# A fused attention and two-layer kernel: the hops of each weight rounding set a point apart, and six w_k blocks moved into the mixing phase

## The chip, the cores and the metric

The kernel runs on one core of a Trainium2 chip. The metric is the device time of one execution in microseconds (us), the median of several runs. The engines are TensorE (PE, matrix products), VectorE (DVE), ScalarE (ACT), GpSimd (POOL) and SyncE (SP, which here only issues DMAs). Each works through its own instructions in program order; semaphores hold one until what it needs from the others is there.

## The reference

The inputs pass through three stages. All matrix products are in fp32 to a tight tolerance.

```python
for t in range(S):                               # delta-rule attention, B=4, H=8, S=768, D=48
    y[:, :, t] = einsum('bhd,bhde->bhe', q[:, :, t], state)
    v_old = einsum('bhde,bhd->bhe', state, kt)
    state = state + bt[:, :, :, None] * einsum('bhd,bhe->bhde', kt, vt - v_old)
h = gelu(x @ w_in); u, v = split(h)              # gated mixing over the sequence
v_n = (v - mean) / sqrt(var + 1e-6) * g_ln
x = x + (u * (einsum('ts,bsd->btd', w_sg, v_n) + b_sg)) @ w_out
k = relu(xk @ w_k); v = k * k @ w_v              # xk, xr: x mixed with x one token earlier
out = sigmoid(xr @ w_r) * v
```

## The kernel before, in words

PE multiplies fp32 numbers as pairs of rounded halves (hi and lo, three products each). The weights arrive as 64-bit floats, so each must first be **rounded**, block by block (128 rows by 192, 256 or 384 columns), by the generator `narrow`: a load of the raw bits (L161, on SP), a cast of the low words (ACT, L165), four DVE operations on the tile `na` (L170, L172, L174, L176), an integer add on POOL (L178), then hi on ACT (L121, in `split`) and lo on POOL (L124). `resident` blocks (12 of w_in) stay in on-chip memory; `scratch` blocks (8 of w_out, 12 of w_k, 3 of w_r, 8 of w_v) are put to DRAM (L203) and loaded again later.

The program has four stages. **Early** (to about 42 us): a triangular solver for the first chunk pair (`solver(0)`, nearly all on DVE) runs, with the first w_in roundings beside it; PE waits for it. **Attention** (to about 345 us): the order on every engine is written out by a planner in Python, one `tick` after the other. A tick's `background` hands DVE time in turn to layer-norm steps, steps of the next solver, and rounding steps of the jobs in `running`; `after(n, f)` puts an instruction n points (ticks) later. Five more solvers run here. Each ends in a transpose (L456) into a tile that the program calls DT, or sw0l where it shares memory, and PE's `couple` (L472) needs it at a set place. **Mixing** (to about 494 us): 32 turns of `mix`, whose product PE makes; DVE scales it (L1072), multiplies it by u (L1074), ACT rounds it (gh, L1075), DVE takes the rest (gl, L1078); `project` multiplies the result by w_out. Some turns also bring in a batch's next v tiles (`to_ring`): ACT rounds one into g (L121), DVE or POOL takes the rest (L124). Between, the function `side` gives two DVE steps a turn to the rounding of w_r and w_v, in up to three blocks at a time, one for each raw buffer of the pool `st`. What is left after the last turn is run off in a loop (`while k == 7 ...`) before the next stage. **Last phase**: `shift` makes the token mix xm (L1165, L1166, L121, L124), and PE computes the third stage chunk by chunk. The tiles of `shift` lie in the memory of that pool, so the first xm_hi waits until the last puts from there have landed.

PE's own instructions stand in the same order in both kernels, so only how long it waits, and its clock, can differ.

## Time and profile before

| what | value |
|---|---|
| runs | 741.00, 735.49, 739.16 us; median 739.16 |
| profiled execution | 737.01 us, of which the span that the trace covers is 735.2 us |
| mean granted PE clock | 0.972 of full speed |
| busy | PE 682.0 us (93%), DVE 502.0 (68%), ACT 364.3 (50%), POOL 202.6 (28%) |
| chain that ended last | PE 78%, DVE 10%, "issue" 4%, ACT 4%, DMA 2% |

The span is what the profiler saw between the first and the last instruction; the 1.8 us around it belong to the execution. A busy share is an average over the whole span. Each engine's instructions are listed with their start, their duration and, in brackets, how long the engine had been idle before and what ended that idle time.

### The profile page before, as it was taken

To read this page: it belongs to the slowest core of one execution; us is meant where nothing else is said; L and a number is where in the kernel's file an instruction comes from. 1 tells how busy PE (TensorE), PEld (TensorE's weight loads), DVE (VectorE), ACT (ScalarE), POOL (GpSimd) and SP (SyncE) were. 2 spreads that over 40 slices of the span, in tenths; PEclk is the share of its full clock that TensorE was granted. 3 is DMA by queue.
4 is the path that set the end of the run, shared out by engine and by line. 5 is a ranking of instruction groups with operands and counts; after the bars stand their busy time and mean duration, and the time that the engine had idled before them with its cause. 6 is when DMAs were issued, how large, how long until landed. Compare 5 with 4: busy or idle time off the path is not lost.

```text
span 735.2 us, 24465 instructions
## 1 busy us (share of the span) xinstructions
PE 682.0 (93%) x10669; PEld 618.3 (84%) x10669; DVE 502.0 (68%) x992; ACT 364.3 (50%) x696; POOL 202.6 (28%) x257
## 2 busy tenths in 40 slices
PE   2568889999997998899999999999999999999998
PEld 2436668878886897789999999998989898999997
DVE  5999989978979695723558676798655564736251
ACT  2235676777765766864322323156444453525140
POOL 4033543454444555643041615330000000000000
PEclk8678999999998999999999999999999999999999
DMA  8402654665665458548853444367000000000000
GB/s 246 108 30 72 158 141 121 177 177 178 155 200 179 126 178 219 186 132 232 284 185 132 153 148 150 109 200 186 33 12 23 22 21 22 18 27 11 33 12 32
DMA packets 80938, 88.71 MB, mean 121 GB/s; under 512 B 24704, under 2 KB 63616, under 8 KB 80832
## 3 DMA queue, kind: packets, MB, share of 16 engines
q1 hardware_dynamic: 75520, 77.33, 35.6%
q0 software_dynamic: 5312, 9.83, 5.0%
q8 instruction: 83, 1.36, 0.8%
q14 instruction: 23, 0.19, 0.1%
HBM read 56.60 MB, written 25.82 MB: 112 GB/s over the span
## 4 chain that ended last, share of the span: by engine, by line
PE 78%; DVE 10%; issue 4%; ACT 4%; DMA 2%; POOL 1%; SPq 1%; ACTq 0%; POOLq 0%; DVEq 0%
PE ms L152 34%; PE ms L976 12%; PE ms L703 7%; PE ms L651 6%; PE ms L579 3%; PE rk L537 2%; PE rk L550 2%; PE rk L514 2%; PE sps L565 2%; PE ms L742 2%; PE ms L334 2%; DVE sg L356 2%; PE ms L472 2%; PE qk L517 1%; DVE sg L396 1%
## 5 line engine op out<-in xcount | busy, mean ns | idle before, releaser
L152 PE MATMUL ms<-wvh,sl 128*128 128x384 f32 x192 | 64.7, 337 | 0.5 <-DVE sl L124 0.5
L152 PE MATMUL ms<-wvh,sh 128*128 128x384 f32 x192 | 64.6, 337 | 0.1
L152 PE MATMUL ms<-wvl,sh 128*128 128x384 f32 x192 | 64.5, 336 | 0.0
L178 POOL TENSOR_TENSOR na<-na,raw 128x256 int32<-128x256 int32 (+2 forms) x43 | 38.7, 899 | 93.3 <-ACT gh L1075 40.7
L1075 ACT ACTIVATE gh<-w 128x384 fp32r<-128x384 f32 x32 | 16.8, 526 | 93.7 <-DVE w L1074 93.7
L152 PE MATMUL ms<-xm_hi,sw0h 128*128 128x512 f32 x144 | 56.1, 390 | 0.0
L152 PE MATMUL ms<-xm_hi,sw0l 128*128 128x512 f32 x144 | 56.1, 389 | 0.0
L152 PE MATMUL ms<-xm_lo,sw0h 128*128 128x512 f32 x144 | 56.0, 389 | 0.0
L124 DVE TENSOR_TENSOR sl<-sg,sh 128x512 fp32r<-128x512 f32 x48 | 33.2, 691 | 28.8 <-ACT sh L121 28.6
L976 PE MATMUL ms<-sw0h,g 128*128 128x384 f32 x192 | 50.2, 335 | 0.0
L976 PE MATMUL ms<-ws1h,g 128*128 128x384 f32 x192 | 49.9, 334 | 0.0
L121 ACT ACTIVATE sh<-sg 128x512 fp32r<-128x512 f32 x48 | 30.3, 631 | 33.9 <-DVE sg L1188 33.9
L1205 DVE TENSOR_TENSOR sg<-sg,ms 128x384 f32<-128x384 f32 x24 | 13.3, 552 | 49.4 <-PE ms L152 49.4
L356 DVE TENSOR_TENSOR sg<-sg,Yt 128x512 f32<-128x512 f32 (+4 forms) x72 | 43.3, 611 | 1.3
L530 POOL TENSOR_SCALAR_AFFINE_SELECT SQ<-SQ 64x512 f32<-64x512 f32 x36 | 28.2, 783 | 48.6 <-ACT SQ L529 47.5
L1187 ACT ACTIVATE sg<-ms 128x512 f32<-128x512 f32 x48 | 28.6, 596 | 26.1 <-PE ms L152 24.1
L1188 DVE TENSOR_TENSOR sg<-sg 128x512 f32<-128x512 f32 x48 | 33.2, 691 | 10.9 <-ACT sg L1187 10.8
L334 PEld LDWEIGHTS ms<-kT 64*32 64x32 f32 x640 | 18.5, 124 | 22.4 <-issue 14.5
L703 PE MATMUL ms<-xl,wiu_hi 128*128 128x256 f32 x144 | 37.0, 296 | 0.0
L152 PEld LDWEIGHTS ms<-wvh,sl 128*128 128x128 f32 x192 | 36.1, 188 | 0.8 <-DVE sl L124 0.8
L703 PE MATMUL ms<-xh,wiu_lo 128*128 128x256 f32 x144 | 36.4, 291 | 0.0
L152 PEld LDWEIGHTS ms<-wvh,sh 128*128 128x128 f32 x192 | 36.1, 188 | 0.4 <-ACT sh L121 0.4
(244 smaller groups left out, 2151.0 us busy)
## 6 DMA issues: line engine op xcount, KB each, us to landing
u_d<-ug SPq DMA_DIRECT2D x24, 256.0 KB, 4.0
u<-u_d SPq DMA_DIRECT2D x16, 384.0 KB, 4.1
vn_d<-v SPq DMA_DIRECT2D x22, 256.0 KB, 3.5
vk<-in_vk_dram SPq DMA_DIRECT2D x24, 192.0 KB, 4.0
vk<-in_vk_dram SPq DMA_DIRECT2D x12, 384.0 KB, 3.7
st<-vn_d SPq DMA_DIRECT2D x18, 256.0 KB, 3.1
out_dram<-sg SPq DMA_DIRECT2D x24, 192.0 KB, 1.9
kT<-in_kt_d_dram SPq DMA_DIRECT2D x8, 512.0 KB, 5.3
```

The lines of the kernel that those rows point to most:

```text
L121: A.activation(hi, src, AF.Copy)
L124: eng_lo.tensor_tensor(lo, src, hi.bitcast(F32), op=ALU.subtract)
L152: T.matmul(pt, lhsT=a, rhs=b, start=(i == 0), stop=(i == n - 1))
L178: G.tensor_tensor(a.bitcast(I32), a.bitcast(I32), w_lo.bitcast(I32), op=ALU.add)
L334: T.matmul(gps[r:r + 32, p, c0:c1], lhsT=t[r:r + 64, u, 0:32], rhs=t[r:r + 64, u, c0:c1], start=True, stop=True)
L356: V.tensor_tensor(tv, vw(a_t, a_off, a_dims), vw(b_t, b_off, b_dims), op=ALU.mult)
L530: G.affine_select(out=pt, in_=pt, pattern=[[0, 8], [1, C]], compare_op=ALU.is_gt, fill=0.0, base=0, channel_multiplier=-1)
L651: T.matmul(vstat[g, b], lhsT=a[:, c], rhs=w[:, c], start=first, stop=last)
L703: T.matmul(vstat["u"][:, 2 * P * d:2 * P * d + 2 * P], lhsT=w[:, c, ds_], rhs=a[:, c].rearrange("p b t -> p (b t)"), start=first, stop=last)
L976: T.matmul(pt[:, :DM], lhsT=v[:, ds_], rhs=w, start=(c == 0 and i == 0), stop=(c == 5 and i == 2))
L1187: A.activation(r, pt, AF.Relu)
L1188: V.tensor_tensor(r, r, r, op=ALU.mult)
```

## The change

It has four parts. First, the hops of a rounding: the POOL add, hi and lo each come one point after the one before, in the early stage and in attention (`hops[0]` is 1), where the add came at once and hi and lo together; in mixing `hops[0]` is 0, so add and lo come without such a pause. Second, rounding jobs get DVE time in the order in which they were begun, all of them and not the first two in turn; up to three run in the early stage (there were two), three in attention (two), and a new one begins every eighth point (sixth). Third, the last six w_k blocks are taken out of the attention stage and rounded in mixing, in a lane of their own that goes ahead of the lane of w_r and w_v. Fourth, the scaling of the second value tile (`scale_v(1)`) has a place at the end of the list of pending work, and pending streams keep their due time when points are counted anew.

```diff
-RUN = (3, 2, 3)
+RUN = (3, 3, 3)
-EVERY = 6
+EVERY = 8
+NMIX = 6
...
-        G.tensor_tensor(a.bitcast(I32), a.bitcast(I32), w_lo.bitcast(I32), op=ALU.add)
+        yield hops[0], lambda: G.tensor_tensor(a.bitcast(I32), a.bitcast(I32), w_lo.bitcast(I32), op=ALU.add)
...
-        yield lag, lambda: split(A, G, af, hi, lo)
+        yield 1, lambda: A.activation(hi, af, AF.Copy)
+        yield hops[0], lambda: G.tensor_tensor(lo, af, hi.bitcast(F32), op=ALU.subtract)
...
-    jobs += j1
+    jobs += j1[:-NMIX]
+    wk_jobs = j1[-NMIX:]
...
-                kinds.append([e for e in ready if any(e[1] is j for _, j in running[:2])])
+                kinds.append([e for _, j in running for e in ready if e[1] is j])
...
-                while len(running) < 2 and len(jobs) > n_rest:
-                    start_job(LJ0 if point[0] else LJ)
+                while len(running) < 3 and len(jobs) > n_rest:
+                    start_job(LJ0 if point[0] else (LJ, LJ, 2 * LJ0)[len(running)])
...
-                after(SV, lambda: scale_v(1))
+                last.append(lambda: scale_v(1))
...
+        for e in streams:
+            e[0] = len(later) if e[0] > point[0] else 0
         point[0] = 0
-        for e in streams:
-            e[0] = 0
+        later += [(len(later) + 1, last[0])]
...
-    jobs += j2 + j3
-    live, turns, starts, owing = [], [0], [4 + 2 * i for i in range(NRAW)], []
+    hops[0] = 0
+    live, turns, owing = [], [0], []
+    lanes = [(jobs + wk_jobs, [0] * NRAW), (j2 + j3, [4 + 2 * i for i in range(NRAW)])]
...
-            while jobs and any(x <= turns[0] for x in starts):
-                starts.remove(next(x for x in starts if x <= turns[0]))
-                j = jobs.pop(0)()
-                next(j)
-                live.append([turns[0] + 2, j, None])
-            e = next((e for e in live if e[0] <= turns[0]), None)
+            for q, starts in lanes:
+                while q and any(x <= turns[0] for x in starts):
+                    starts.remove(next(x for x in starts if x <= turns[0]))
+                    j = q.pop(0)()
+                    next(j)
+                    live.append([turns[0] + 2, j, None, starts])
+            e = next((e for _, x in lanes for e in live if e[0] <= turns[0] and e[3] is x), None)
...
-        while k == 7 and (live or jobs):
+        while k == 7 and (live or lanes[1][0]):
```

**ACT in the early stage.** L343 (L345 after) are the four copies of the first Gram product out of PSUM into sg1, which solver 0's first transpose on DVE needs whole; L165 (L164) is the cast of a raw block, L121 (L181) its hi. Before:

```order
L165 ACTIVATE raw_145<-raw_145 128x256
L165 ACTIVATE raw_147<-raw_147 128x256
L343 ACTIVATE sg1_109<-ms_234 128x8x32
L121 ACTIVATE wiv_hi_91<-na_227 128x256
L121 ACTIVATE wiv_hi_91<-na_229 128x256
L343 ACTIVATE sg1_109<-ms_281 128x8x32
```

After:

```order
L164 ACTIVATE raw_145<-raw_145 128x256
L345 ACTIVATE sg1_109<-ms_233 128x8x32
L164 ACTIVATE raw_147<-raw_147 128x256
L345 ACTIVATE sg1_109<-ms_273 128x8x32
L181 ACTIVATE wiv_hi_91<-na_228 128x256
L345 ACTIVATE sg4_112<-ms_315 128x256
```

The fourth copy into sg1 stood behind two hi's, which wait for POOL's adds; now it stands ahead of both.

**DVE at the end of solver 4** (the one whose result TensorE waits for longest). L491 (L493) adds up a chunk's residual r32 and waits for PE; L356 and L396 (L358, L398) are products and sums of the solver; L170 to L176 (L169 to L175) belong to a rounding. Before:

```order
L491 TENSOR_TENSOR r32_4582<-vk_3871,rk_4546 128x384
L356 TENSOR_TENSOR sg3_111<-sg2_110,Yt_144 128x512
L356 TENSOR_TENSOR sg3_111<-sg2_110,Yt_144 128x256
L396 TENSOR_REDUCE sg2_110<-sg3_111 128x4x16
L670 BN_STATS st6_4606<-v_4593 128x6
L356 TENSOR_TENSOR sg3_111<-sg2_110,Yt_144 128x768
L170 TENSOR_SCALAR na_4613<-raw_4597 128x256
L396 TENSOR_REDUCE sg2_110<-sg3_111 128x4x16
L172 TENSOR_SCALAR na_4613<-na_4613 128x256
```

After:

```order
L358 TENSOR_TENSOR sg3_111<-sg2_110,Yt_144 128x512
L358 TENSOR_TENSOR sg3_111<-sg2_110,Yt_144 128x256
L398 TENSOR_REDUCE sg2_110<-sg3_111 128x4x16
L493 TENSOR_TENSOR r32_4542<-vk_3835,rk_4506 128x384
L169 TENSOR_SCALAR na_4558<-raw_4431 128x192
L358 TENSOR_TENSOR sg3_111<-sg2_110,Yt_144 128x768
L171 TENSOR_SCALAR na_4558<-na_4558 128x192
L672 BN_STATS st6_4566<-v_4553 128x6
L398 TENSOR_REDUCE sg2_110<-sg3_111 128x4x16
```

Two products and a sum of the solver that came behind the residual (L356 with 512 and 256 columns and the first L396) come ahead of it; a block of 192 columns stands where one of 256 stood.

**ACT at the end of mixing.** L1075 (L1080) is the last turn's gh, L121 (L181) a block's hi, L165 (L164) a cast, xm_hi the first instruction of the last phase that waits for the blocks' puts. Before:

```order
L1075 ACTIVATE gh_8024<-w_8083 128x384
L1165 ACTIVATE sg1_8167<-xT_63,m1_sb_66 128x512
L1165 ACTIVATE sg2_8168<-xT_63,m1_sb_66 128x512 x2
L1075 ACTIVATE gh_8024<-w_8109 128x384
L121 ACTIVATE raw_7973<-na_8033 128x384
L121 ACTIVATE xm_hi0_8220<-sg1_8167 128x512 x2
```

After:

```order
L1080 ACTIVATE gh_7990<-w_8079 128x384
L181 ACTIVATE raw_7938<-na_7999 128x384
L181 ACTIVATE raw_7940<-na_8057 128x384
L164 ACTIVATE raw_8084<-raw_8084 128x384
L181 ACTIVATE raw_8084<-na_8141 128x384
L164 ACTIVATE raw_8137<-raw_8137 128x384
L181 ACTIVATE raw_8137<-na_8151 128x384
L120 ACTIVATE xm_hi0_8220<-sg1_8167 128x512 x2
```

One block was open behind the last gh; now four are, of which two are not yet cast.

**SP at the end of mixing.** L161 (L160) loads a raw block of w_v, L203 puts a rounded one to DRAM. Before:

```order
L203 DMA wv_d_6887<-raw_7619 128x768
L161 DMA raw_7973<-in_w_v_dram 128x768
L203 DMA wv_d_6887<-raw_7747 128x768
L203 DMA wv_d_6887<-raw_7897 128x768
L203 DMA wv_d_6887<-raw_7973 128x768
```

After:

```order
L160 DMA raw_8084<-in_w_v_dram 128x768
L203 DMA wv_d_6815<-raw_7938 128x768
L160 DMA raw_8137<-in_w_v_dram 128x768
L203 DMA wv_d_6815<-raw_7940 128x768
L203 DMA wv_d_6815<-raw_8084 128x768
L203 DMA wv_d_6815<-raw_8137 128x768
```

The last load stood ahead of the last three puts and had its buffer early. Now the load of raw_8137 stands behind the put of raw_7938, whose buffer it takes over, and waits until that put has landed.

## Rows read from the trace of the kernel before

**Rows 1.** Windows: bounds, length, busy PE, PEld, DVE, ACT, POOL (instructions), PE clock, DMA, GB/s

```profile
80.00:340.00 260.00, 242.97 (x6747) 209.59 (x6739) 199.50 (x427) 177.63 (x347) 126.25 (x166) 0.98 0.60 167
232.80:238.00 5.20, 5.16 (x77) 4.91 (x78) 4.83 (x22) 2.35 (x5) 0.89 (x2) 0.50 0.57 180
340.00:490.00 150.00, 150.00 (x868) 149.27 (x867) 102.36 (x181) 46.78 (x91) 48.54 (x50) 1.00 0.55 177
```

**Rows 2.** Timeline of ACT and DVE, 10 to 16 us: start, duration, instruction, [idle before <- releaser]

```profile
13.82 0.42 ACT L121 ACTIVATE wiv_hi<-na 128x256 fp32r<-128x256 f32 x1 [1.53 <-POOL na L178]
14.14 0.80 ACT L343 ACTIVATE sg<-ms 128x256 f32<-128x256 f32 x2
...
10.50 0.75 DVE L176 SCALAR_TENSOR_TENSOR na<-raw,na 128x256 uint32<-128x256 uint32 x2
14.76 1.25 DVE L361 STREAM_TRANSPOSE sg<-sg 128x1024 f32<-128x1024 f32 x1 [3.51 <-ACT sg L343]
```

**Rows 3.** Timeline of TensorE, 36 to 49 us

```profile
41.97 6.50 PE L742 MATMUL ms<-warm 128*128 128x512 bf16 x18 [5.55 <-DVE warm L452]
```

**Rows 4.** Waits of TensorE, 80 to 345 us: total us, times, longest

```profile
PE ms L472 <- DVE sw0l L456: 3.4, 2, 3.1
PE ms L472 <- DVE DT L456: 1.9, 1, 1.9
...
PE ms L651 <- ACT ug L707: 1.4, 1, 1.4
PE ms L579 <- ACT SQ L556: 1.3, 2, 1.1
```

**Rows 5.** Timeline of DVE, then TensorE, 220 to 235 us

```profile
220.56 0.55 DVE L491 TENSOR_TENSOR r<-vk,rk 128x384 f32<-128x384 f32 x1 [2.70 <-PE qk L517]
221.03 1.48 DVE L356 TENSOR_TENSOR sg<-sg,Yt 128x512 f32<-128x512 f32 x2
222.43 0.67 DVE L396 TENSOR_REDUCE sg<-sg 128x64 f32<-128x512 f32 x1
...
230.85 1.93 DVE L456 STREAM_TRANSPOSE sw0l<-sg 128x1024 f32<-128x1024 f32 x1
...
232.84 1.92 PE L472 MATMUL ms<-sw0l,sw0h 32*32 32x32 f32 x64 [3.08 <-DVE sw0l L456]
```

**Rows 6.** Timeline of ACT, POOL and TensorE, 486 to 495 us

```profile
486.53 0.51 ACT L121 ACTIVATE raw<-na 128x384 fp32r<-128x384 f32 x1
490.96 2.19 ACT L121 ACTIVATE xm_hi<-sg 128x512 fp32r<-128x512 f32 x4 [3.93 <-DMA wv_d<-raw]
...
487.11 1.42 POOL L124 TENSOR_TENSOR raw<-na,raw 128x384 fp32r<-128x384 f32 x1 [3.79 <-ACT raw L121]
...
494.32 0.39 PE L152 MATMUL ms<-xm_hi,sw0h 128*128 128x512 f32 x1
```

**Rows 7.** Chain of waits, 478 to 500 us: start, duration, what

```profile
488.56 2.30 DMA wv_d<-raw
```

**Rows 8.** DMA issues of the span: count, size, median us to landing

```profile
raw<-in_w_v_dram SPq DMA_DIRECT2D x8, 384.0 KB, 3.2
```

**Rows 9.** Windows of the tile na alone: busy us of DVE, ACT, POOL (instructions)

```profile
80.00:340.00 260.00, 40.32 (x92) 9.47 (x24) 37.67 (x48) 0.98 0.60 167
340.00:495.00 155.00, 19.93 (x44) 5.63 (x11) 24.27 (x22) 1.00 0.55 175
```

**Rows 10.** Timeline of DVE, POOL and TensorE, 368 to 382 us

```profile
369.94 1.64 DVE L1078 TENSOR_TENSOR gl<-w,gh 128x384 fp32r<-128x384 f32 x1
...
374.99 0.62 DVE L1072 SCALAR_TENSOR_TENSOR w<-ms,g_sb,b_sb 128x384 f32<-128x384 f32 x1 [0.60 <-PE ms L976]
...
377.31 0.69 DVE L124 TENSOR_TENSOR g<-st,g 128x512 fp32r<-128x512 f32 x1
...
368.31 2.86 POOL L124 TENSOR_TENSOR g<-st,g 128x512 fp32r<-128x512 f32 x2 [18.79 <-ACT g L121]
...
380.86 0.51 PE L976 MATMUL ms<-sw0h,g 128*128 128x384 f32 x2
```

More of the change, by code (lines that the diff above doesn't have):

```diff
@@ L34 @@
 WARM = 4
-SV = 60
 B0 = 1.0
@@ L39 @@
 SOLVE0 = 1
-RUN = (3, 2, 3)
+RUN = (3, 3, 3)
 SUMS = (0,)
-EVERY = 6
+EVERY = 8
+NMIX = 6
 LATE = 100
 PUT = 2
-JLAG = 2
 BUDGET = 1.62
@@ L153, in mm3, with narrow @@
                 i += 1
-    def narrow(dram, i, j, hi, lo, cw=CW, pool=stg, lag=JLAG, parts=None):
+    def narrow(dram, i, j, hi, lo, cw=CW, pool=stg, parts=None):
         w = CW if pool is stg else cw
@@ L190, in resident @@
         return hi, lo, [lambda i=i, j=j: narrow(dram, i, j, hi[:, i, j - j0:j - j0 + CW],
-                                                lo[:, i, j - j0:j - j0 + CW], lag=0)
+                                                lo[:, i, j - j0:j - j0 + CW])
                         for i in range(nblk) for j in range(j0, j1, CW)]
@@ L221, in fused_kernel @@
     wk_dh, wk_dl, j1 = scratch(w_k, "wk", 3, FF)
-    jobs += j1
+    jobs += j1[:-NMIX]
+    wk_jobs = j1[-NMIX:]
     n_rest = len(jobs)
+    hops = [1]
     fp = tc.tile_pool(name="fp", bufs=2)
@@ L819, in fused_kernel @@
                  ((st_n, 0, 0), (st_rq, 1, 0)), ((st_d, 1, 0), (st_s, 0, 0), (st_y, 0, 0))]
-        rest = [lambda j=j: whole(j) for j in diag[4:]]
+        last, rest = [], [lambda j=j: whole(j) for j in diag[4:]]
         k = 0
@@ L1044, in side @@
                 live.remove(e)
-                starts.append(turns[0] + 1)
+                e[3].append(turns[0] + 1)
             elif isinstance(c, tuple) and c[0]:
@@ L1126, in fused_kernel @@
         if k == 6:
+            assert not lanes[0][0] and all(e[3] is not lanes[0][1] for e in live)
             wk = [[None] * 3 for _ in range(2)]
```

## The prediction

> **What bounds the kernel now.** I read the windows first, since the busy shares of the whole span mix stages with different limits. In mixing PE is busy all of the time, 150.00 of 150 us, with DVE at 102.36 [rows 1]: nothing that the other engines gain there shortens anything, and they have to take on a good deal before it costs. From 80 to 340 us PE is busy 242.97 of 260 us, so some 17 us are idle and can be won at most, besides what the clock loses. Before about 42 us PE waits for solver 0 on DVE; the last wait of that stage is 5.55 us, for a DVE instruction inside the solver [rows 3]. So the question of this change is which waits before 340 us it shortens, and what six more blocks do to a mixing stage that had no wait, and to the handover behind it.
>
> The waits from 80 to 345 us name few places [rows 4]: the solver's last transpose (3.4 us in two waits, and 1.9 in one more) and ACT evictions behind others (1.4 and 1.3). The longest, 3.08 us, ends at 232.84 [rows 5]. In the 5.2 us after it PE runs at a granted clock of 0.50, its lower level of 1.2 GHz, and is busy 5.16 of them [rows 1]; at 2.4 GHz that work is 2.6 us. The wait and what the clock did after it cost 3.1 + 2.6 = 5.7 us.
>
> **Early stage.** The solver's first transpose starts at 14.76, when the two last copies into sg have come out of ACT. They stand behind a hi that waited 1.53 us for POOL's add [rows 2]. With the new order the last of them that the transpose needs stands ahead of both hi's. DVE has nothing else then but the rounding that ends at 10.50 + 0.75 = 11.25; the transpose follows a part of it, so I let it begin at 10.6 instead of 14.76, 4.1 us earlier (11.25 would make it 3.5). Against it, the add and lo of the blocks now run beside the solver, which before had waited for them. I take 1.0 us off, from the row of a DVE instruction that ran beside POOL, 1.64 us [rows 10], against 0.69 for a similar one without [rows 10]: one such meeting. **Gain 3.1 us**, bounds 1.5 (three meetings) and 4.1.
>
> **Six blocks fewer in attention.** A block costs DVE four instructions of 40.32 / 92 = 0.44 us, so six are 10.5 us less in the stage, and about 6 x (2 x 0.78) = 9.4 us less of POOL and 6 x 0.39 = 2.4 of ACT [rows 9]. What of it reaches PE is decided at the places where it waits.
> - Solver 4: the residual waits for PE at 220.56, after 2.70 us of DVE idle time [rows 5]. Two products (1.48) and a sum (0.67) that came behind it now fill part of this idle time: 2.15 us earlier. The rounding between has 192 columns instead of 256, a quarter off 4 x 0.44, which is 0.4. That makes 2.6 of the 3.08 us, and what of the wait stays would then be short enough to leave open whether the clock falls. The full price is 5.7, and if only the 2.6 come off and the clock still falls it is 2.6. I take **5.0**, near the full price, because DVE stands idle there for longer than the moved work takes; bounds 1 and 5.7.
> - The other wait on that tile: 3.4 - 3.08 = **0.3** us [rows 4, 5], bounds 0 and 0.3; with fewer DVE steps ahead of it I let it go.
> - Solver 5: its last stretch holds as many rounding steps as before, so its wait of 1.9 [rows 4] stays: **0**, bounds -1 (the transpose comes later as three blocks run at once) and +1.9.
> - From 283 to 330 us: the ACT waits of 1.4 and 1.3 [rows 4] come while rounding instructions queue on ACT and POOL; two blocks fewer there and hops that wait less on ACT: **2.0**, bounds 0 and 2.7.
>
> Together **10.4 us** (with 3.1 from the early stage), bounds 1.5 and 14.7.
>
> **Mixing.** Lane 0 adds 6 x 4 = 24 DVE instructions of 19.93 / 44 = 0.45 us [rows 9], or 10.9 us, to a DVE with 47.6 us free. But it adds them early: twelve of them now stand ahead of the DVE instruction at 377.31, which makes the lo of a v tile, g, that PE first reads with the second of the two products that start at 380.86, so at about 381.0 [rows 10]. Twelve are 5.4 us; the idle 0.60 at 374.99 absorbs that much. The lo is ready at 377.31 + 0.69 + 5.4 - 0.6 = 382.8, or 1.8 us late. Part of DVE's free time must lie ahead of 374.99 too, so I take **1.0** late; bounds 0 and 8.3 (a rival below).
>
> **The handover.** This is the loss that the order shows and no row of before has. In before one block was open behind the last gh: hi at 486.53, lo at 487.11, its put at 488.56 for 2.30 us, and xm_hi at 490.96 after 3.93 us of waiting [rows 6, 7]. PE noticed nothing, since `project` kept it busy until xm was ready at 494.32 [rows 6]. After the change lane 0 has taken the turns that the last two blocks would have used. Behind the last gh, at the same place on ACT, stands the hi of raw_7938, and the load of raw_8137 needs this buffer. So, one after the other: hi 486.53 + 0.51, lo 1.10, put 2.30, load 3.2 [rows 8], four DVE instructions 1.81, add 1.10, hi 0.51, lo 1.10, put 2.30 [rows 6 to 9]; 1.10 is 24.27 / 22. The sum is 13.9 us, and the eight handovers at 0.03 to 0.10 us each (487.11 - 487.04, 490.96 - 490.86) make 0.6. xm_hi can start at 486.53 + 13.9 + 0.6 = 501.0, its first 0.55 us (2.19 / 4) done at 501.6. PE then waits from 494.32 to 501.6, or 7.3 us. Afterwards the clock: 3.08 us of waiting were followed by 5.2 us at 0.50 [rows 1, 5], and I charge the same 2.6 here. **Loss 9.9 us.** Lower bound 6.5, with POOL at its quick end, no slow put, and a clock that recovers at once; upper bound 13, with lo at 1.42 twice [rows 6], load and put a microsecond longer each, and a second stretch at the lower level. The loads of w_r and w_v that wait for the last put are wanted a whole chunk of products later, and I let them cost nothing; if that cover failed they would cost the 3 us or so by which they are late.
>
> The Trainium skill (DMA: Bandwidth & Descriptors, "Anatomy of one DMA") states a fixed part of about 2.0 us for one DMA and a size part of its bytes over 436,000 a microsecond. By it (an estimate from that page) each 384 KB transfer of the chain is 2.9 us, three of them 8.7 where the rows give 7.8, and the loss would be 10.8; the rows decide here, 2.30 and 3.2.
>
> **Sum.** On the profiled execution 737.01: -10.4 + 1.0 + 9.9 = +0.5, so 737.5. That execution lies 2.15 under the median of the runs; moved over to the median 739.16 it is 739.7, and I give **739.5**.
>
> **Rivals.** *Faster: the handover costs its lower bound and the gains come in full.* 6.5 against gains of some 15: DVE's relief takes the whole 3.08 and the clock stretch, and the 1.9 of solver 5 and its aftermath too. -14.7 + 1.0 + 6.5 = -7.2, or 732. For it: DVE is what most of these waits name [rows 4], and 10.5 us of it go. Against: the last stretch of solver 5 has not changed.
>
> *Slower: DVE and POOL block each other in the first mixing turns.* Five more POOL instructions now run before the g split. At 369.94 a DVE instruction took 1.64 us while POOL ran two splits from 368.31 [rows 10]; the longer one at 377.31 took 0.69, so each meeting may cost 1.0. Five make the g split about 5 us later than at best: PE waits some 5.7 us at 381, and at the price above 2.6 more for the clock, 8.3 in place of 1.0. That gives 739.7 + 7.3 = 747. It decides from the third such meeting on, when the wait passes 3 us; for fewer it is hidden in my bounds. Against it: DVE has idle time on both sides of this stretch [rows 1], and POOL's hops here wait for ACT, which thins them out.
> The Trainium skill (SBUF — State Buffer, "Who interferes with whom") says that a DVE instruction with two SBUF inputs contends with a GpSimd instruction that reads SBUF, and that the loser is blocked for the whole instruction. By that rule this rival is the likelier in mixing; the trace agrees at 369.94 only, as far as it shows.
>
> *The change does less than it says:* the waits at solvers 4 and 5 stay, since the transpose waits for something else, and gains are 4; then -4 + 1.0 + 9.9 = +6.9, or 746. I count it with the slower side.
>
> **How the numbers follow.** A measurement of this kernel can tell about 1%, or 7.4 us, from no change. The forecast, gains and losses that nearly cancel: 0.53. The faster rival and what lies beyond it: 0.26. The two slower ones: 0.21, of which a good half passes 1%, but so do combinations of the upper bound of the handover with middling gains. The range of 730 to 747 reaches to both rivals' own times and leaves a tenth out on either side.
>
> **What would show it.** In the profile after: a wait of some 7 us of PE on xm_hi near 500 us (shifted earlier by the gains), with a chain of put, load, DVE, POOL, put before it, and a granted clock of 0.5 behind it; the transpose of solver 0 some 4 us earlier; no wait, or a short one, on the solver 4 transpose and no stretch at 0.50 there; a short wait on DVE's lo of g at the first batch change in mixing. The prediction is wrong if the wait for xm_hi is under 4 us, if the early stage gains nothing, or if PE waits in mixing by more than 3 us.

## The result and the profile after

The changed kernel takes 745.15 us in the median (741.84 to 748.53, nine runs) against 739.16 for the kernel before in the same measurement. The ratio is 1.0076, with a 95% interval of 1.0049 to 1.0103: slower by a little under 1%. The forecast was 739.5, the range 730 to 747. The profiled execution after took 745.61 us, with a span of 743.8 at a mean granted clock of 0.970.

PE's matmuls stand in the same order in both kernels, and either trace holds 10,669 of them. So the two traces can be laid side by side: the start of a matmul after, minus the start of the same matmul before, says how much has been lost or won up to that place. This **shift** is +0.9 us when solver 0's wait ends (42 us), -4.2 at 92, -1.4 at 128, -2.4 at 225, -4.0 at 345, -0.4 from 382 to 494, +9.7 at 498 and +8.6 from 520 to the end. So in these two executions 4.0 us are won before mixing, 3.7 of them are given back in mixing, and 9.0 are lost at the handover. The sum of +8.6 is between two single executions; that of before, 737.01 us, was a quick one, and the medians differ by 6.0.

**The handover.** The windows of the kernel after (bounds, length, then busy PE, PEld, DVE, ACT and POOL with instructions, PE clock, DMA, GB/s) show where the loss is; the first answers to the last window of [rows 1].

```profile
340.00:490.00 150.00, 147.09 (x851) 146.06 (x850) 106.83 (x197) 46.76 (x96) 52.67 (x52) 1.00 0.55 181
...
496.00:507.00 11.00, 5.93 (x14) 4.43 (x15) 4.64 (x9) 5.33 (x10) 4.59 (x6) 0.53 0.94 258
```

From 496 to 507 us PE is busy 5.93 of 11 us. The chain of waits of the kernel after (start, duration, what) tells what it waits for, link by link:

```profile
489.25 3.22 DMA raw<-in_w_v_dram
...
492.56 0.37 DVE na L169
...
493.35 0.97 DVE na L173
...
495.27 1.00 POOL na L177
...
496.90 1.00 POOL raw L182
...
497.92 2.36 DMA wv_d<-raw
...
500.38 0.64 ACT xm_hi L120
```

This is the forecast chain: load, DVE, add, lo, put, xm_hi. Its first links stand on SP's timeline, where the put of the buffer is issued at 486.85 and the load that takes this buffer over only at 489.25, when the put has landed. The end of the chain on the timelines of ACT and TensorE (after the duration, in brackets, the idle time before and what ended it) answers to the xm_hi rows of [rows 6]:

```profile
500.38 2.19 ACT L120 ACTIVATE xm_hi<-sg 128x512 fp32r<-128x512 f32 x4 [3.56 <-DMA wv_d<-raw]
...
501.07 0.80 PE L151 MATMUL ms<-xm_hi,sw0h 128*128 128x512 f32 x1 [6.94 <-ACT xm_hi L120]
```

PE waited 6.94 us (forecast: 7.3). From 496 to 507 the mean granted clock is 0.53, and the same xm matmul takes 0.80 us where it took 0.39 [rows 6]. From 495 to 498 the shift grows by 10.1, of which 3.0 is the clock, and 1.1 comes back by 518, where before had small waits of its own: 9.0 in all.

**Mixing.** Two waits are new. The first was in no part of the prediction. DVE, then TensorE:

```profile
360.42 0.30 DVE L169 TENSOR_SCALAR na<-raw 128x256 uint32<-128x256 uint32 x1 [3.61 <-DMA raw<-in_w_k_dram]
...
360.96 0.61 DVE L1077 SCALAR_TENSOR_TENSOR w<-ms,g_sb,b_sb 128x384 f32<-128x384 f32 x1
...
364.50 0.55 DVE L1083 TENSOR_TENSOR gl<-w,gh 128x384 fp32r<-128x384 f32 x1
...
365.10 0.45 PE L151 MATMUL ms<-gl,wo_hi 128*128 128x384 f32 x1 [1.62 <-DVE gl L1083]
```

The first rounding step of lane 0 comes due before its load has landed. DVE works in order, so for 3.61 us it does nothing, and the scaling of the mixing turn (L1077) behind that step stands too; its gl reaches PE 1.62 us late. The second wait is the forecast one, on the lo of g. POOL, DVE, TensorE:

```profile
378.77 3.23 POOL L123 TENSOR_TENSOR g<-st,g 128x512 fp32r<-128x512 f32 x2 [3.02 <-ACT g L120]
...
379.08 1.77 DVE L123 TENSOR_TENSOR g<-st,g 128x512 fp32r<-128x512 f32 x1
...
380.91 0.62 PE L979 MATMUL ms<-sw0h,g 128*128 128x384 f32 x2 [1.24 <-DVE g L123]
```

DVE's lo of g begins 1.8 us later than in [rows 10] and takes 1.77 us beside POOL's two, where it took 0.69.

**Before mixing.** The waits of TensorE from 80 to 340 us (us in all, times, longest), beside [rows 4]:

```profile
PE ms L474 <- DVE DT L458: 3.5, 3, 1.5
PE ms L653 <- ACT ug L709: 3.0, 2, 2.3
PE ms L474 <- DVE sw0l L458: 2.3, 1, 2.3
```

Solver 4's wait (sw0l) is 2.3 where it was 3.1, and a wait on ug that [rows 4] has only at 1.4 now has a 2.3 in it. That one is new, at 251.5 us: POOL, ACT, TensorE.

```profile
247.94 1.48 POOL L483 TENSOR_TENSOR vk<-vk,neT 128x768 f32<-128x768 f32 x1 [3.86 <-DMA vk<-in_vk_dram]
249.37 1.18 POOL L177 TENSOR_TENSOR na<-na,raw 128x256 int32<-128x256 int32 x1
...
250.58 0.42 ACT L181 ACTIVATE raw<-na 128x256 fp32r<-128x256 f32 x1 [5.23 <-POOL na L177]
250.90 0.58 ACT L709 ACTIVATE ug<-ms 128x512 f32<-128x512 f32 x1
...
251.54 0.50 PE L653 MATMUL ms<-wiv_hi,xh 128*128 128x512 f32 x1 [2.26 <-ACT ug L709]
```

Put a point later, the add of a block (L177) now stands on POOL behind the scaling of a value tile (L483), which itself waits 3.86 us for a DMA. The block's hi on ACT waits 5.23 us for the add, and the eviction that PE needs (ug) stands behind the hi.

In the early stage the rows that answer to [rows 2] and [rows 3] are, of TensorE, ACT, DVE and TensorE:

```profile
13.72 0.21 PE L338 MATMUL ms<-kT 64*32 64x32 f32 x1 [4.82 <-issue]
...
14.44 0.63 ACT L345 ACTIVATE sg<-ms 128x256 f32<-128x256 f32 x1 [4.47 <-PE ms L338]
...
15.11 1.25 DVE L363 STREAM_TRANSPOSE sg<-sg 128x1024 f32<-128x1024 f32 x1 [3.19 <-ACT sg L345]
...
42.86 3.43 PE L744 MATMUL ms<-warm 128*128 128x512 bf16 x8 [5.33 <-DVE warm L454]
```

The copy stands ahead of both hi's now, as the order said, but it waits for PE: the last piece of the first Gram product comes at 13.72. The transpose starts at 15.11 (before 14.76), and PE's wait for solver 0 ends at 42.86 (before 41.97).

### The profile page after: what moved, and what is told of

It reads as the page before. It is cut to its first block, busy times and chain, and to the rows that moved or that the text cites. A ratio compares the mean times of both kernels' runs of the same rounds, so it can differ in the third digit from the quotient of the medians.

```text
span 743.8 us, 24469 instructions
## 1 busy us (share of the span) xinstructions
PE 682.0 (92%) x10669; PEld 618.6 (83%) x10669; DVE 508.0 (68%) x992; ACT 363.9 (49%) x696; POOL 205.2 (28%) x257
## 4 chain that ended last, share of the span: by engine, by line
PE 67%; DVE 20%; DMA 5%; issue 4%; ACT 2%; SPq 1%; POOL 1%; ACTq 0%; DVEq 0%; POOLq 0%
PE ms L151 36%; PE ms L979 8%; PE ms L705 6%; PE ms L653 5%; DVE sg L358 4%; DVE sg L398 2%; PE ms L581 2%; PE rk L539 2%; PE sps L567 2%; PE rk L552 1%; PE rk L516 1%; DMA vk<-in_vk_dram 1%; PE ms L336 1%; DVE Yt L398 1%; PE ms L474 1%
## 5 line engine op out<-in xcount | busy, mean ns | idle before, releaser
L177 POOL TENSOR_TENSOR na<-na,raw 128x256 int32<-128x256 int32 (+2 forms) x43 | 38.2, 889 | 107.2 <-DVE na L175 61.8
L1080 ACT ACTIVATE gh<-w 128x384 fp32r<-128x384 f32 x32 | 16.8, 526 | 90.6 <-DVE w L1079 90.6
L1211 DVE TENSOR_TENSOR sg<-sg,ms 128x384 f32<-128x384 f32 x24 | 13.3, 552 | 51.2 <-PE ms L151 51.2
L532 POOL TENSOR_SCALAR_AFFINE_SELECT SQ<-SQ 64x512 f32<-64x512 f32 x36 | 30.6, 850 | 51.3 <-ACT SQ L531 50.1
L358 DVE TENSOR_TENSOR sg<-sg,Yt 128x512 f32<-128x512 f32 (+4 forms) x72 | 41.6, 590 | 1.5
L1194 DVE TENSOR_TENSOR sg<-sg 128x512 f32<-128x512 f32 x48 | 33.2, 691 | 12.8 <-ACT sg L1193 12.7
L151 PEld LDWEIGHTS ms<-xm_hi,sw0h 128*128 128x128 f32 x144 | 27.7, 192 | 12.9 <-ACT xm_hi L120 7.3
L338 PE MATMUL ms<-kT 64*32 64x64 f32 (+1 forms) x640 | 22.2, 229 | 17.3 <-issue 17.2
L345 ACT ACTIVATE sg<-ms 128x256 f32<-128x256 f32 x32 | 17.6, 578 | 40.9 <-PE ms L338 40.7
```

The costliest lines, as they stand in the source:

```text
L151: T.matmul(pt, lhsT=a, rhs=b, start=(i == 0), stop=(i == n - 1))
L177: yield hops[0], lambda: G.tensor_tensor(a.bitcast(I32), a.bitcast(I32), w_lo.bitcast(I32), op=ALU.add)
L358: V.tensor_tensor(tv, vw(a_t, a_off, a_dims), vw(b_t, b_off, b_dims), op=ALU.mult)
L532: G.affine_select(out=pt, in_=pt, pattern=[[0, 8], [1, C]], compare_op=ALU.is_gt, fill=0.0, base=0, channel_multiplier=-1)
L1194: V.tensor_tensor(r, r, r, op=ALU.mult)
```

## The experiments

The theory after the result: the handover costs some 9 us and is set by how many DVE steps are left after turn 31; the gain before mixing comes from the hops and not from the six blocks; the two waits in mixing come from the place of lane 0's first steps. Each rival says that the same time hangs on the blocks themselves. The table has the shift against the kernel before (between two profiled executions, us) where the same matmul starts at these times before, and the ratio of the times.

| kernel | 128 | 225 | 249 | 345 | 382 | 494 | end | ratio [95%] |
|---|---|---|---|---|---|---|---|---|
| after | -1.4 | -2.4 | -2.9 | -4.0 | -0.4 | -0.4 | +8.6 | 1.0076 [1.0049, 1.0103] |
| 1 no move | -3.9 | -2.6 | -4.0 | -0.6 | +1.8 | +1.8 | +1.8 | 1.0000 [0.9973, 1.0027] |
| 2 three steps | -2.9 | -3.1 | -7.5 | -7.6 | -4.2 | -2.0 | -3.1 | 0.9951 [0.9921, 0.9982] |
| 3 move alone | -0.5 | +0.7 | +1.5 | +0.2 | +3.4 | +3.4 | +11.6 | 1.0091 [1.0059, 1.0124] |
| 4 two early | -1.2 | +0.5 | -3.1 | -0.6 | +3.8 | +3.8 | +12.8 | 1.0104 [1.0068, 1.0139] |
| 5 add at once | +1.3 | +0.1 | -2.0 | -2.5 | +0.8 | +0.8 | +9.1 | 1.0099 [1.0063, 1.0136] |
| 6 mixing mended | -2.3 | -2.6 | -6.9 | -6.3 | -6.3 | -0.4 | +4.5 | 1.0047 [1.0023, 1.0071] |
| 7 both mended | +1.9 | +1.3 | -2.4 | -3.3 | -3.3 | +2.6 | +6.9 | 1.0059 [1.0029, 1.0089] |
| 8 hops alone | -4.7 | -3.0 | -2.6 | +1.8 | +2.2 | +2.2 | +3.9 | 1.0049 [1.0013, 1.0084] |
| 9 three steps, late add at once | +2.1 | +3.6 | -0.3 | -1.1 | +3.1 | +5.3 | +4.2 | 0.9945 [0.9920, 0.9971] |
| 10 all mended | -2.5 | -0.3 | -4.3 | -5.3 | -5.3 | +4.4 | +3.4 | 0.9983 [0.9957, 1.0009] |

A shift is of one execution, against one quick execution of the kernel before. Executions of one kernel differ by 4 to 11 us (kernel 9: 733.55 to 741.10, and its profiled one is the slowest of twelve). How far a shift can stray shows where kernels have the same instructions in the same order on every engine. The changed kernel and kernels 2, 6, 9 and 10 have them up to 240 us, and their shifts at 225 are -2.4, -3.1, -2.6, +3.6 and -0.3; kernel 3 has those of the kernel before up to 249 us, and its shift there is +1.5. The granted clock differs between such executions: from 40 to 60, 60 to 80 and 80 to 100 us it was 0.83, 1.00 and 1.00 in kernel 2, and 0.74, 0.91 and 0.83 in kernel 9. So shifts are read here for where they jump, and the ratios for what a kernel is worth.

**1. No blocks moved.** The changed kernel with all twelve w_k blocks in attention again, one beginning every sixth point as before.

```diff
-EVERY = 8
+EVERY = 6
...
-    jobs += j1[:-NMIX]
-    wk_jobs = j1[-NMIX:]
+    jobs += j1
+    wk_jobs = []
```

> The changed kernel without its third part: all twelve w_k blocks stay in attention, a new job begins at every sixth point again; hops, order, three jobs and the rest stay. My theory (the loss of the change is all in mixing and the handover, 3.7 and 9.0 us in its trace, and the 4.0 us won before 340 us come from hops and order): no wait for gl or g in mixing, none for xm_hi, and about 735, ratio 0.994. Rival (the 4.0 us come from the six blocks that attention is rid of): 739, ratio 1.000 to before.

Measured: 741.00 us, ratio 1.0000. The ratio is the rival's and not the theory's 0.994, which lies outside the interval. There is no wait on xm_hi, so the handover belongs to the move. The shift is -3.9 at 128 us, -2.6 at 225 and -4.0 at 249 without any block moved. But the wait on ug at 251 us is longer here (3.30 us, with a granted clock of 0.62 from 251.5 to 256), and at 345 the gain is nearly gone (-0.6). In mixing the wait on gl came all the same, for 1.63 us, from the one block that was left over: DVE stood 3.06 us for that block's load. So that wait is a matter of one early step whose load has not landed, not of how many steps there are.

**2. Three steps a turn from turn 8 on.** One line of the changed kernel, so that the lanes are done before the last turn.

```diff
-        side(SD)
+        side(SD + (turns[0] >= 8))
```

> The changed kernel with three DVE steps of rounding a turn instead of two from the ninth turn of mixing on, so that no block is left behind the last turn. My theory (the 9.0 us are the chain through the buffer of the last blocks, which is there only because steps are left over): the wait for xm_hi and the stretch at the lower clock behind it are gone, the two waits early in mixing stay, 745.1 - 9.0 = 736, ratio 0.996. Rival (DVE then makes the later v tiles late): new waits of 1 to 3 us on g in the later batches, 739 to 742.

Measured: 736.39 us, ratio 0.9951. The wait on xm_hi is gone, and the ratio falls by 0.0125, or 9.2 us. This is the price of the handover, measured by taking it away, less what the third step costs in mixing: 2.2 us in the trace (the shift goes from -4.2 at 382 to -2.0 at 494, half of it at a wait of 0.89 us on gl at 487). ACT and TensorE at the handover:

```profile
489.05 2.19 ACT L120 ACTIVATE xm_hi<-sg 128x512 fp32r<-128x512 f32 x4 [3.39 <-DMA wv_d<-raw]
...
492.32 0.39 PE L151 MATMUL ms<-xm_hi,sw0h 128*128 128x512 f32 x1
```

xm_hi still waits 3.39 us for a put, but PE is kept busy by `project` until 492.32, as before the change. The waits on gl and on g at the start of mixing stay (1.62 and 1.25), and that on ug too (2.36).

**3. The move alone.** The kernel before, with nothing but the lane of six w_k blocks in mixing (the body of `side` as in the diff of the change).

```diff
-    jobs += j1
+    jobs += j1[:-6]
+    wk_jobs = j1[-6:]
...
-    live, turns, starts, owing = [], [0], [4 + 2 * i for i in range(NRAW)], []
+    live, turns, owing = [], [0], []
+    lanes = [(jobs + wk_jobs, [0] * NRAW), (j2 + j3, [4 + 2 * i for i in range(NRAW)])]
```

> The kernel before with the third part alone: six w_k blocks in a lane of their own in mixing, hops, order and number of jobs as before. My theory: the waits in mixing and the handover come as in the changed kernel, +3.7 + 9.0, and attention gains little from fewer blocks: 750, ratio 1.015. Rival (the relief of DVE is the gain): 4 us less, 747 or under, ratio 1.010.

Measured: 748.91 us, ratio 1.0091. Again the ratio is the rival's (1.010), and the theory's 1.015 lies outside the interval. Up to 249 us the instructions are those of the kernel before, so the shift of +1.5 there, and solver 4's wait of 4.2 us where [rows 5] has 3.08, are of the execution. From 249 to 345 us the shift goes from +1.5 to +0.2, so the trace shows 1.3 us won by the six blocks. The time speaks for more: it is 6.7 us above before, where the trace loses 11.4 behind 345 us, and that leaves some 4.7 won ahead of it. In mixing and at the handover the losses are those of the changed kernel, with waits of 1.4 on gl and 1.3 on g. The waits of TensorE from 200 us on:

```profile
PE ms L152 <- ACT xm_hi L121: 6.9, 1, 6.9
PE ms L473 <- DVE sw0l L457: 4.2, 1, 4.2
```

**4. Two jobs in the early stage.** The changed kernel with two early rounding jobs where it has three.

```diff
-                while len(running) < 3 and len(jobs) > n_rest:
-                    start_job(LJ0 if point[0] else (LJ, LJ, 2 * LJ0)[len(running)])
+                while len(running) < 2 and len(jobs) > n_rest:
+                    start_job(LJ0 if point[0] else LJ)
```

> The changed kernel with two rounding jobs in the early stage as before, not three. Theory: the third job's load, which stands ahead of the others on SP, makes PE's instructions come later, so that its idle time before the fourth piece of the first product was 4.82 instead of 2.78 us; with two jobs that piece starts at about 12.3, the solver's first transpose at 13.7 instead of 15.1, and the time is 1.4 us less, 743.7. Rival: the idle time has another cause, the piece starts at 13.7 again and the time is unchanged, 745.

Measured: 749.78 us, ratio 1.0104. TensorE and DVE:

```profile
12.07 0.19 PE L338 MATMUL ms<-kT 64*32 64x32 f32 x1 [2.85 <-issue]
...
13.25 1.25 DVE L363 STREAM_TRANSPOSE sg<-sg 128x1024 f32<-128x1024 f32 x1 [1.89 <-ACT sg L345]
...
27.30 0.29 DVE L169 TENSOR_SCALAR na<-raw 128x256 uint32<-128x256 uint32 x1 [2.28 <-DMA raw<-in_w_in_dram]
```

The Gram piece comes at 12.07 and the transpose 1.5 us earlier than before the change, so the third load is what delays PE there: up to 39 us only SP's instructions differ from those of the changed kernel. It is so in every kernel of the table: with two early loads the piece starts at 12.07 (kernels 3, 4 and 8; 12.33 before), with three at 13.4 to 15.4 (all eight others). But the 1.5 us are then lost inside solver 0, where DVE stands 2.28 us for the next block's load. PE's wait ends no earlier (a shift of +1.7 at 42 us), and the 1.4 us of the theory are not won.

**5. The add at once.** The changed kernel with the POOL add issued without its hop, as before; hi and lo keep theirs.

```diff
-        yield hops[0], lambda: G.tensor_tensor(a.bitcast(I32), a.bitcast(I32), w_lo.bitcast(I32), op=ALU.add)
+        G.tensor_tensor(a.bitcast(I32), a.bitcast(I32), w_lo.bitcast(I32), op=ALU.add)
```

> The changed kernel with the POOL add again right behind the DVE steps in every stage; hi and lo keep their hop. Theory (the hop puts one add behind the scaling of a value tile on POOL, which waits for its DMA and for PE; a hi on ACT waits for that add, and the eviction of ug behind it holds PE for 2.3 us at 251 us, with a stretch of lower clock in some runs): that wait is gone, and with it 2 to 4 us, 742, ratio 1.003 to before. Rival (PE then waits for something else at the same place, such as the vk tile itself): no difference to the changed kernel, 1.0076.

Measured: 746.11 us, ratio 1.0099. The wait on ug at 251 is gone (the shift stays at -2.0 from 249 to 273 us, where the changed kernel goes from -2.9 to -0.6). The shift at 128 us is +1.3, with three waits of TensorE; the changed kernel has at these places 0.69 us on r and nothing else:

```profile
58.14 0.88 PE L539 MATMUL rk<-r,sw0l 32*32 32x48 f32 x64 [1.61 <-ACT r L491]
...
65.52 1.04 PE L552 MATMUL rk<-u,sg 32*32 32x48 f32 x32 [1.97 <-ACT u L544]
...
106.71 1.27 PE L539 MATMUL rk<-r,DT 32*32 32x48 f32 x64 [2.34 <-DVE r L493]
```

The first two, on ACT's r and u, come again in kernel 7 (0.83 and 1.22 us), which has the same instructions to there, and no kernel with the hop has more than the 0.69; the third is no matter of the hop, since kernel 2 has 1.37 us there. So one and the same hop shortens two waits before 130 us and makes one at 251. What it is worth in sum can't be told from nothing: the intervals of the two ratios overlap.

**6. The start and the end of mixing mended.** In the changed kernel the first blocks of lane 0 come due at turn 4 instead of 2, and the two turns d = 0 and 1 of each group of four have three steps from turn 8 on.

```diff
-                    live.append([turns[0] + 2, j, None, starts])
+                    live.append([turns[0] + (2 if turns[0] else 4), j, None, starts])
...
-        side(SD)
+        side(SD + (turns[0] >= 8 and d < 2))
```

> The changed kernel with mixing mended: the first three blocks get their first DVE step at the fifth turn, not the third, when their loads have landed, and from the ninth turn on two of four turns have three steps, so that nothing is left behind the last turn. Theory (the wait of 1.62 us for gl at 365 us comes from DVE standing behind a load of w_k that has not landed, that of 1.24 us for g from twelve more steps ahead of it, the 9.0 from the handover): all three go, 745.1 - 9.0 - 2.9 = 733, ratio 0.992. Rival (the steps only move the waits to the later batches, as one of 0.9 us did with three steps in every turn): 735 to 737, ratio 0.996.

Measured: 744.50 us, ratio 1.0047, above the theory's 0.992 and the rival's 0.996. The waits at the start are both gone: the shift stays at -6.3 from 345 to 411 us. So the place of lane 0's first steps made both. Then the steps that had been put off stood ahead of the next split of g. DVE, POOL, TensorE:

```profile
412.38 1.20 DVE L169 TENSOR_SCALAR na<-raw 128x384 uint32<-128x384 uint32 x1
413.61 1.30 DVE L171 TENSOR_SCALAR na<-na 128x384 f32<-128x384 f32 x1
414.84 1.75 DVE L123 TENSOR_TENSOR g<-st,g 128x512 fp32r<-128x512 f32 x1
...
413.31 2.73 POOL L123 TENSOR_TENSOR g<-st,g 128x512 fp32r<-128x512 f32 x2
...
416.64 0.62 PE L979 MATMUL ms<-sw0h,g 128*128 128x384 f32 x2 [3.38 <-DVE g L123]
```

Three DVE instructions that take 0.35, 0.35 and 0.69 us alone take 4.25 beside POOL's add and splits. PE waits 3.38, and from 417 to 421 us the granted clock is 0.57: 5.4 us in all. A block is left over at the end too, and xm_hi costs 2.6. What had been mended, 3.7 us in the changed kernel, came back in another turn at 5.4.

**7. Both mended.** Kernel 6 with the add at once, as in 5.

```diff
-        yield hops[0], lambda: G.tensor_tensor(a.bitcast(I32), a.bitcast(I32), w_lo.bitcast(I32), op=ALU.add)
+        G.tensor_tensor(a.bitcast(I32), a.bitcast(I32), w_lo.bitcast(I32), op=ALU.add)
```

> Both mends together: the add at once, and mixing as in the run beside it. If the two losses are independent: 1.0076 - 0.004 - 0.016 = 0.988, 730. If the wait at 251 us only hid another one: the same as the run with mixing mended alone, 0.992.

Measured: 744.88 us, ratio 1.0059. The two edits add up as they are: no wait on ug, those of kernel 5 before 130 us, 3.38 us on g, 2.61 on xm_hi; and 1.77 us at 295. Nothing is won over kernel 6.

**8. The hops alone.** The kernel before with the hops of add, hi and lo, and nothing else of the change.

```diff
-        G.tensor_tensor(a.bitcast(I32), a.bitcast(I32), w_lo.bitcast(I32), op=ALU.add)
+        yield hops[0], lambda: G.tensor_tensor(a.bitcast(I32), a.bitcast(I32), w_lo.bitcast(I32), op=ALU.add)
...
-        yield lag, lambda: split(A, G, af, hi, lo)
+        yield 1, lambda: A.activation(hi, af, AF.Copy)
+        yield hops[0], lambda: G.tensor_tensor(lo, af, hi.bitcast(F32), op=ALU.subtract)
```

> The kernel before with the first part alone: add, hi and lo a point apart; order of jobs, their number and the w_k blocks as before. It tells where the 4 us that the changed kernel had won by 90 us come from. If from the hops: 4 us less by 90 us, and, with the wait for ug at 250 us if a scaling meets an add there, 737 to 741 in all, 0.994 to 1.0. If from the order and the number of jobs: nothing by 90 us, 741 or above, ratio 1.0 to 1.005.

Measured: 744.74 us, ratio 1.0049. By the time the hops alone win nothing; they make the kernel 0.5% slower, and the interval excludes 1. Its profiled execution, 740.74, is quicker than this median; in it the shift is -4.7 at 128 us and -3.0 at 225, and from there to 345 us 4.8 are lost, among others in a wait of the same kind as that on ug:

```profile
271.75 0.42 ACT L182 ACTIVATE raw<-na 128x256 fp32r<-128x256 f32 x1 [4.94 <-POOL na L178]
...
273.27 1.15 PE L581 MATMUL ms<-SQ 128*64 128x64 f32 x32 [2.79 <-ACT v L662]
```

A hi stands on ACT for 4.94 us until POOL's add comes, and evictions stand behind it.

**9. Three steps, and the late adds at once.** Kernel 2, with the add's hop only up to point 96 of attention, so that it is gone at 251; up to 240 us every engine has its instructions in the order of kernel 2.

```diff
-        yield hops[0], lambda: G.tensor_tensor(a.bitcast(I32), a.bitcast(I32), w_lo.bitcast(I32), op=ALU.add)
+        yield hops[0] * (point[0] < 96), lambda: G.tensor_tensor(a.bitcast(I32), a.bitcast(I32), w_lo.bitcast(I32), op=ALU.add)
...
-        side(SD)
+        side(SD + (turns[0] >= 8))
```

> The kernel with three steps a turn from turn 8, and the POOL add without its hop from point 96 of attention on (its hop stays before). Theory: the add's hop wins its 4 us before about 130 us, and costs one wait of 2.3 us on ug near 250 us, because the add then stands on POOL behind the scaling of the second value tile, which waits for a DMA. So the early gain stays (a shift of about -4 near 128 us against the kernel before), the wait near 247 falls below 0.5, and the time is some 2.4 us below the one with three steps alone: about 734, ratio 0.991, no xm_hi wait. Rival: the wait near 250 belongs to the scaling itself and stays, or the add, at once again, holds another wait of about 2 us between 130 and 340 (as the kernel with the add at once everywhere had before 130): then 736 to 737, ratio 0.995 as with three steps alone.

Measured: 735.56 us, ratio 0.9945 [0.9920, 0.9971]. The wait on ug is gone by the mechanism that was named: the add stands ahead of the scaling (L483) on POOL, and the hi waits 0.61 us instead of 5.23.

```profile
247.86 0.74 POOL L177 TENSOR_TENSOR na<-na,raw 128x256 int32<-128x256 int32 x1
250.95 1.48 POOL L483 TENSOR_TENSOR vk<-vk,neT 128x768 f32<-128x768 f32 x1 [2.35 <-PE sps L567]
...
248.64 0.42 ACT L181 ACTIVATE raw<-na 128x256 fp32r<-128x256 f32 x1 [0.61 <-POOL na L177]
```

Against the profiled execution of kernel 2 PE gains 2.4 us between 237 and 249. The time does not show it: the ratio is 0.0006 below that of kernel 2, within either interval. In the traces they are lost again: the shift lies 7.2 us above that of kernel 2 at 240 us, 4.7 at 252, 6.5 at 345 and 7.3 at 382. The rival's second wait is among what is lost: PE stands 1.66 us at 291.60, against 0.58 at the same place in kernel 2, and kernels 5, 7 and 10, whose add comes at once there too, have waits of 1.93, 1.77 and 1.57 between 290 and 296 us. The 7 us that this execution lies behind that of kernel 2 were lost before 95 us, with the same instructions and a lower granted clock.

**10. All mended.** Kernel 9 with the first blocks of lane 0 due at turn 4.

> As the run beside it, and in mixing the first blocks of lane 0 come due two turns later, so that DVE does not reach one whose load has not landed. Theory: the wait on gl near 361 to 365 (1.6 us) is that load's and goes, so 1.5 us below the run beside it, ratio 0.989. Rival: in-order DVE only moves its stand: the steps put off fall into the turns ahead of the next split of a v tile (turn 16), whose g comes late by 3.4 us with a granted clock of 0.50 behind it, as in the kernel with the mixing mended: then some 4 us above the run beside it, ratio about 0.996, with a wait on g of over 2 us near 417 us.

Measured: 740.23 us, ratio 0.9983. As the rival said, the stand moves: the waits at the start of mixing go (the shift stays at -5.3 from 345 to 382 us), then two waits come in which the steps that were put off are in DVE's way, with a granted clock of 0.57 from 418 to 422 us and from 493 to 497. TensorE:

```profile
415.91 0.44 PE L979 MATMUL ms<-sw0h,g 128*128 128x384 f32 x1 [1.46 <-ACT g L120]
...
491.85 0.44 PE L151 MATMUL ms<-gl,wo_hi 128*128 128x384 f32 x1 [1.70 <-DVE gl L1083]
```

The first is shorter than the rival had it (1.46, not over 2) and on ACT's part of g. With smaller ones beside them they take the shift from -5.3 to +4.4.

## Why the prediction was right, and where its terms were not

**The whole.** 745.15 lies in the range and within 1% of before, the likeliest case. It is 5.6 us above the forecast. In the traces the forecast sum was +0.5 and came to +8.6: the gains 4.0 instead of 10.4, mixing 3.7 instead of 1.0, the handover 9.0 instead of 9.9. The two large misses add up, and the range, 17 us wide, held them; of the large terms only the handover came at its size in this execution. The third rival (the change does less than it says: gains of 4, 746) has nearly the time and the gains of this execution, but not its reason: the waits at solvers 4 and 5 did not stay, they fell (3.08 to 2.29, and 1.9 to 1.5). Two of the three signs of being wrong bear on this. The early stage gained nothing, which by the prediction's own words makes it wrong there; PE's two waits in mixing are 2.86 us, just under the 3 of the last sign, with 3.7 lost in all.

**The handover: right, in mechanism and size.** Forecast 9.9, measured 9.0 between the traces and 9.2 by kernel 2, which pays 2.2 in mixing for it. The chain is the one that was read from the order of ACT and SP. It began 1.8 us earlier than forecast (hi of the reused buffer at 484.73, not 486.53) and took 15.7 us instead of 14.5, so xm_hi came at 500.38 instead of 501.0. The wait was 6.94 (forecast 7.3), the clock 3.0 (forecast 2.6). The put took 2.36 and the load 3.22, near the 2.30 and 3.2 of [rows 7] and [rows 8]. The Trainium skill (DMA: Bandwidth & Descriptors, "Anatomy of one DMA") states its fixed part and its size part for DMAs that GpSimd issues, and these are issued on SP. The estimate of 2.9 us that the prediction worked out from it is near half of one put and one load (5.6), but neither transfer is near it.

**The early stage: wrong.** The step "the last of them that the transpose needs stands ahead of both hi's ... so I let it begin at 10.6 instead of 14.76" took for granted that only ACT's order held the transpose. The copy had a second holder that came right behind the first: PE's last Gram piece, at 12.33 already before, which bounds the transpose at about 13.3 (12.07 and 13.25 in kernel 4). TensorE before:

```profile
12.33 0.19 PE L336 MATMUL ms<-kT 64*32 64x32 f32 x1 [2.78 <-issue]
```

The third early load moved this piece to 13.72. And in kernels 4 and 8, with two early loads, even an earlier transpose won nothing: DVE then stands 2.28 and 1.32 us for the next load. Forecast -3.1, measured +0.9. By the prediction's own test ("if the early stage gains nothing") it fell here.

**Solver 4: the mechanism held, and the profiled execution hides most of its size.** "Near the full price" of 5.7 was taken as 5.0. In the profiled execution the wait fell only from 3.08 to 2.29, the clock behind it was 0.67, and from 225 to 240 us the shift moves by 1.6. But DVE's stretch from the residual to PE's couple became 2.17 us shorter: 10.11 (219.50 to 229.61) where it was 12.28 (220.56 to 232.84 [rows 5]). That is the 2.15 of the two products and the sum, and nothing of the 0.4 for the narrower block, one step of which took 1.44 us beside POOL's scaling: I had not priced the POOL instruction beside it. Kernels 2, 6, 9 and 10 have the same instructions up to there and the same 10.1 us of DVE. In them the wait is 0.94, 0.94, 1.46 and 1.23, the granted clock in the 5.2 us behind it 1.00, and from 225 to 249 us the shift falls by 4.4, 4.3, 3.9 and 4.0. So in four of five executions this term came near its forecast; why PE reached the wait earlier in the fifth is not shown. The changed kernel (DVE, POOL, TensorE, window), then kernel 2 (TensorE, window):

```profile
219.50 0.55 DVE L493 TENSOR_TENSOR r<-vk,rk 128x384 f32<-128x384 f32 x1 [2.75 <-PE qk L519]
...
222.56 1.44 DVE L173 TENSOR_SCALAR na<-na 128x192 uint32<-128x192 uint32 x1
...
222.41 1.47 POOL L483 TENSOR_TENSOR vk<-vk,neT 128x768 f32<-128x768 f32 x1
...
229.61 1.46 PE L474 MATMUL ms<-sw0l,sw0h 32*32 32x32 f32 x64 [2.29 <-DVE sw0l L458]
...
229.60:234.80 5.20, 5.19 (x103) 4.80 (x107) 4.82 (x19) 2.23 (x5) 0.85 (x2) 0.67 0.22 75
...
227.61 1.20 PE L474 MATMUL ms<-sw0l,sw0h 32*32 32x32 f32 x64 [0.94 <-DVE sw0l L458]
...
227.60:232.80 5.20, 5.19 (x178) 4.82 (x180) 4.82 (x20) 3.09 (x7) 1.97 (x4) 1.00 0.33 104
```

**The six blocks and the hops before mixing: not separated.** The theory after the result gave the whole gain to the hops, and the times speak against it. Without the move the ratio is 1.0000 (kernel 1), with the hops alone 1.0049 (kernel 8), and the relief by six blocks is worth between 1.3 us by kernel 3's trace and some 4.7 by its time. In kernel 1, where no block is moved, DVE's stretch at solver 4 is 11.08 us instead of 10.11, and the wait 2.42.

**The hops: what they do by themselves was not priced.** The prediction has no term for them before 130 us. There they shorten the waits on r and u that kernels 5 and 7 have; that this is a gain of some 4 us is not shown, since kernels with the same instructions differ by 5.0 us at 128 (-2.9 in kernel 2, +2.1 in kernel 9). What a hop does also differs by block. In the kernel before, hi and lo of the w_out and w_k blocks already came two points behind the add (`JLAG = 2`), so there the add and lo come a point later and hi stays; those of w_in came with the add, so there hi comes two points later and lo three. Nor has the prediction a term for the wait that the hops bring at 251. That wait costs 2.3 us, more than the 2.0 forecast as a gain for 283 to 330, and of the two waits there that were to go, 1.4 and 1.1, 0.8 and 1.1 are still there.

**Mixing: the named wait at its size, another not seen.** The lo of g was forecast 1.0 late and came 1.2 late. The wait on gl (1.62) comes from a load not yet landed (kernels 1 and 6). The prediction counted lane 0's DVE steps, but not when their loads land, although the code shows the first step two turns behind its load (`turns[0] + 2`). Forecast +1.0, measured +3.7, of which the two waits are 2.9 and smaller ones the rest.

**The slower rival,** DVE and POOL in each other's way at the first g, had its mechanism but not its number: one meeting (1.77 us instead of 0.69) and not three. At the next g, in kernel 6, three came together, and the price was 5.4 us. The Trainium skill (SBUF — State Buffer, "Who interferes with whom") names two kinds of DVE instruction that contend with POOL: those with two SBUF inputs, and copies, casts and tensor_scalars in a mode that uses both ports. The prediction drew on the first alone. The trace agrees with both as far as it goes, since it does not name the mode: the lo of g was stretched to 1.77 and 1.75, and the rounding steps with one input (L169, L171, L173) to 1.20, 1.30 and 1.44 us.

**What stays open.** How the hops, the order and number of jobs, and the six blocks share what is won before mixing, since the second and the fourth part of the change were run in no kernel by themselves; where kernel 8 loses 4.8 us between 225 and 345 apart from the wait at 273; and whether kernel 9 is any quicker than kernel 2. Both beat the kernel before by 0.5%, and kernel 2 is the changed kernel with one line more.

## What to carry to other kernels

When work is moved behind other work, price first the place where the moved work ends: a pool whose buffers the next stage waits for turned six blocks in an idle engine into 9 us, and one more step a turn gave them back. Where an engine works in order, a step whose load may not have landed costs everything behind it, however idle the engine looks (3.6 us here); and before a wait is counted as a gain, look for the holder that comes second, since the transpose moved no more than the 1.5 us that PE's piece left, and DVE then stood for a load. And before a difference between two traces is given to a cause, look at two executions of the same instructions: here they lie up to 6.7 us apart at 225 us, more than the gain that was to be explained.

## What the runs showed of the hardware

- With a third 256 KB load begun in the first 5 us, PE's last Gram piece began at 13.4 to 15.4 us in eight kernels, with two at 12.07 to 12.33 in four; the profile names "issue", that is nothing that it shows, as what PE waited for (4.82 against 2.78 us). What ties the load to PE there is not shown.
- DVE instructions beside POOL ones were stretched also with one input: the 128 x 192 steps from 0.25 (L169 at 219.97 after) to 1.44 us beside POOL's 1.47, the 128 x 384 steps from 0.35 to 1.20 and 1.30 beside an add and two splits. A block's four DVE steps are no fixed price.
- After a wait of 1.46 or 1.70 us in mixing the granted clock was 0.57 from 418 to 422 and from 493 to 497 us (kernel 10), while the wait of 1.62 at 365 us was followed by no lower clock (1.00 over 340 to 490 us in the kernel after).
- The granted clock is not a property of the instructions alone: kernels 2 and 9, the same up to 240 us, had 0.83, 1.00, 1.00 and 0.74, 0.91, 0.83 from 40 to 60, 60 to 80 and 80 to 100 us, and solver 4's wait was followed by 0.67 in the changed kernel and by 1.00 in the four others with its instructions.
